# The gate of a mixture-of-experts layer computed with tokens as weights and 8 moving columns

## The chip, the cores and the metric

The kernel runs on one NeuronCore of one Trainium2 chip. The metric is device time in microseconds, the median of several runs. TensorE multiplies matrices (its loads of weights are shown as an engine of their own, PEld, since they overlap its products), VectorE (DVE) and ScalarE (ACT) work on elements, GpSimd (POOL) too, and SyncE (SP) issues DMAs.

## The reference

An attention with two kinds of local mask gives 2304 tokens of 512 channels. A mixture of 8 experts follows, whose weights P come from a gate, and then a squared-ReLU layer. The part that the change touches is the gate:

```python
def _moe_ref(x, w_gate, w1, w2):
    N, D = x.shape                      # 2304, 512
    E = w_gate.shape[1]                 # 8
    logits = x @ w_gate
    logits = logits - logits.max()
    P = np.exp(logits)
    for _ in range(8):
        P /= P.sum(1, keepdims=True) + 1e-09
        P /= P.sum(0, keepdims=True) + 1e-09
        P *= N / E
    out = np.zeros((N, D), dtype=np.float32)
    for e in range(E):
        h = np.maximum(x @ w1[e], 0.0)
        ye = h @ w2[e]
        out += P[:, e:e + 1] * ye
    return out
```

## The kernel before

The attention's output stays in SBUF as `xf`, with the channels on the partitions: 128 partitions, 4 channel tiles (`KC`), 2304 tokens, in float32. The attention is a software pipeline of 28 slots (`slot`, line 754). In slot i TensorE gets the scores of group i (`s`, line 297), the products with the values of group i-3 (`xt`, line 349), the transposes of group i-2 (`pt`, line 334) and then a few filler products (`warm_up`, line 752, 128x512). ScalarE copies `xt` out of PSUM into `xf` (line 377), and the next slot's `xt` products wait for those copies, as there are two PSUM buffers.

Every engine's queue has the order in which the code is written (`manual_schedule`); no planner reorders it. The gate is a generator: each `next` records one piece. In the attention loop a gate over 512 tokens is made in slots 10, 16 and 22, so its first piece stands behind the fillers of that slot, and its second piece behind the fillers of the next slot. The tokens from 1536 on have two more gates, of 512 and 256 tokens, after the loop: their pieces stand around the first two units of the expert stage (`l1_pair`, whose products are line 477).

A gate's first piece computes the logits with the channels' gate weights loaded: for each of the 4 channel tiles the 8 gate columns, padded to 32, are the weights, and 512 tokens move. The four products go to four strips of 32 partitions of one PSUM bank, so there are four partial sums with the expert on the partition. VectorE copies the bank to SBUF (`lt`). The second piece transposes 128 tokens at a time with `ident`, and VectorE adds the four partial sums in one reduction into `ptile`, which has a token on each partition and 18 x 8 logits behind it. `sinkhorn` reads `ptile`; its steps are recorded after the units of the first expert steps, and one of its products, line 435, has a 128x128 matrix of ones as weights and 8 moving columns in float32.

The rest of the kernel, from some 117 us on, is a long sequence of expert and feed-forward products (lines 477, 604, 635) that neither the gate nor the change touches.

Of the kernel before, what the change touches and what calls it, by code (L numbers as in the profile page):

```python
# [9 lines left out]
F32 = mybir.dt.float32  # L10
# [4 lines left out]
ALU = mybir.AluOpType  # L15
AX = mybir.AxisListType
# [4 lines left out]
E, FE, FF = 8, 1024, 2048  # L21
# [9 lines left out]
KC = DM // 128  # L31
# [16 lines left out]
def tile_kernel(ctx: ExitStack, tc: tile.TileContext, a):  # L48
    nc = tc.nc
    out = a["out"]  # L50
# [8 lines left out]
    xfp = att.enter_context(tc.tile_pool(name="xfp", bufs=1))  # L59
    qkv = att.enter_context(tc.tile_pool(name="qkv", bufs=2))  # L60
    at = att.enter_context(tc.tile_pool(name="at", bufs=2))
# [7 lines left out]
    ptile = big.tile([128, NCH, E], F32, name="ptile")  # L69

    xf = xfp.tile([128, KC, NTOK], F32, name="xf")

    ident = const.tile([128, 128], F32, name="ident")
    mask = xfp.tile([128, 4 * GB, KB], F32, name="mask")
    wg = xfp.tile([128, KC, 32], F32, name="wg")
    warm = xfp.tile([128, 128], F32, name="warm")
    guard = xfp.tile([128, GB, 1], F32, name="guard")

# [5 lines left out]
    bufs = {"s": 2, "xt": 2, "pt": 1, "mm": 3}  # L84

    def bank(tag):
        return psum.tile([128, 512], F32, tag=tag, name=tag, bufs=bufs[tag])
# [290 lines left out]


    def gate(t0, n):  # L380
        ps = bank("mm")
        for kc in range(KC):
            nc.tensor.matmul(
                ps[32 * kc:32 * kc + 32, :n], wg[:, kc], xf[:, kc, t0:t0 + n], start=True, stop=True
            )
        lt = at.tile([128, 512], F32, tag="lt", name="lt", bufs=1)
        nc.vector.tensor_copy(lt[:, :n], ps[:, :n])
        yield
        ps2 = bank("mm")
        nch = n // 128  # L390
        for c in range(nch):
            nc.tensor.transpose(ps2[:, c * 128:(c + 1) * 128], lt[:, c * 128:(c + 1) * 128], ident)
        c0 = t0 // 128
        nc.vector.tensor_reduce(
            out=ptile[:, c0:c0 + nch, :],
            in_=ps2[:, :n].rearrange("p (c k q) -> p c q k", k=KC, q=32)[:, :, :E, :],
            axis=AX.X,
            op=ALU.add,
        )
        yield  # L400

    def sinkhorn():
# [272 lines left out]
    with tc.manual_schedule():  # L675
# [14 lines left out]
        ps = psum.tile([128, 512], F32, tag="s", name="s")  # L690
# [88 lines left out]
        for i in range(NG + LAG):  # L779
            slot(i)  # L780
            if i % per == LAG and i > per:
                t = i // per - 1
                gates.append(gate(t * 512, 512))
            if gates:
                try:
                    next(gates[0])
                except StopIteration:
                    gates.pop(0)
            for i0, z in ops:
                if i >= i0:  # L790
                    next(z, None)
            if per + 2 <= i and prep0:
                prep0.pop(0)()
            if i == 3 * per + LAG:
                nc.sync.dma_start(x_dram[:, :, :early], xf[:, :, PAIRS[1]:3 * S])
# [7 lines left out]
        )  # L803
        first_units = l1_pair(0)
        gates += [gate(t0, n) for t0, n in ((1536, 512), (2048, 256))]
        next(gates[0])
        run(first_units[0])
# [70 lines left out]
def _layout(x):  # L878
    q, k, v = x["q"], x["k"], x["v"]

    def order(z):
        lo = z[:, :4]
        hi = z[:, 4:].reshape(B, 4, S // DIL, DIL, D).transpose(0, 1, 3, 2, 4).reshape(B, 4, S, D)
        return np.stack([lo, hi], axis=1)

    qo, ko, vo = order(q), order(k), order(v)

    def pairs(z):
        return z.reshape(B, 2, 2, 2, S, D).transpose(0, 1, 3, 5, 2, 4)

    qs = pairs(qo).reshape(B, 2, 128, 2, NM, QC).transpose(0, 1, 4, 2, 3, 5)
    kz = pairs(ko).reshape(B, 2, 128, 2, S)
    kz = np.concatenate([np.zeros((B, 2, 128, 2, PAD), kz.dtype), kz], axis=-1)
    ks = np.stack([kz[..., m * QC:m * QC + KCOLS] for m in range(NM)], axis=2)

    vp = np.concatenate([np.zeros((B, 2, 4, PAD, D), v.dtype), vo], axis=3)
    vt = np.stack([vp[:, :, :, j * QB:j * QB + KB] for j in range(NB)], axis=3)
    vt = vt.reshape(B, 2, 4, NM, 2, GB // 2, KB, D).transpose(0, 1, 3, 4, 6, 5, 2, 7)
    vt = vt.reshape(B, 2, NM, 128, GB // 2, 4 * D)

    def first(w, n):
        return w.reshape(KC, 128, n, FC, 128).transpose(2, 1, 3, 0, 4).reshape(n, 128, KC * FB)

    def second(w, n):
        return w.reshape(n, FC, 128, DM).transpose(0, 2, 1, 3).reshape(n, 128, FC * DM)

    w1 = np.concatenate([first(x["moe_w1"][e], SPE) for e in range(E)])
    w2 = np.concatenate([second(x["moe_w2"][e], SPE) for e in range(E)])
    kk = np.arange(KB)[None, :]
    qq = np.arange(QB)[:, None]  # L910
    band = (kk > qq) & (kk <= qq + PAD)

    def split_at(o):
        return band & ((qq < o) | (kk >= PAD + o))

    first_block, split, after_split = split_at(0), split_at(QB // 2), band & (kk >= QB // 2)
    masks = [
        z[3 * (k % 2) + k // 2]
        for z in (
            [first_block] + [band] * 5,  # L920
            [first_block, band, band, band, split, after_split],
            [band, band, band, first_block, band, band],
            [band, split, after_split, band, band, band],
        )
        for k in range(GB)
    ]
    arrays = {
        "q": qs,
        "k": ks,
        "v": vt,  # L930
        "w_gate": np.pad(x["moe_w_gate"].reshape(KC, 128, E).transpose(1, 0, 2), ((0, 0), (0, 0), (0, 32 - E))),
        "w1": w1,
        "w2": w2,
        "w_in": first(x["moe2_w_in"], NS2),
        "w_out": second(x["moe2_w_out"], NS2),
        "mask": np.tile(np.stack([np.where(m, 0.0, NEG).astype(np.float32) for m in masks], axis=1), (4, 1, 1)),
        "ident": np.eye(128, dtype=np.float32),
    }
    arrays = {n: np.ascontiguousarray(z) for n, z in arrays.items()}
    for n in ("w_in", "w_out"):  # L940
        arrays[n] = arrays[n].view(np.int64)
    return arrays
# [16 lines left out]
```

## Time and profile before

| | |
|---|---|
| median of 3 runs | 2044.98 us (2043.14 to 2047.37) |
| the profiled execution | 2052.68 us |
| its span, first to last instruction | 2050.9 us |
| TensorE: products, of the span | 2017.1 us, 98% |
| TensorE: loads of weights | 1663.0 us, 81% |
| VectorE | 1558.3 us, 76% |
| ScalarE | 720.4 us, 35% |
| GpSimd | 386.6 us, 19% |
| mean granted clock of TensorE | 0.993 of full speed |

The profile is of one execution. An engine's busy time counts the stretches in which it has an instruction in flight. Products are pipelined: the time from one's start to the start of the next says more of the pace than the length of one. A float32 product of the gate or of the attention shows two records of loads and two of products, so four of the gate's products read x8. The granted clock has two levels here, 2.4 GHz (1.00) and 1.2 GHz (0.50).

### The profile page before, as it was taken

To read this page: it belongs to the slowest core of one execution; us is meant where nothing else is said; L and a number is where in the kernel's file an instruction comes from. 1 tells how busy PE (TensorE), PEld (TensorE's weight loads), DVE (VectorE), ACT (ScalarE), POOL (GpSimd) and SP (SyncE) were. 2 spreads that over 40 slices of the span, in tenths; PEclk is the share of its full clock that TensorE was granted. 3 is DMA by queue.
4 is the path that set the end of the run, shared out by engine and by line. 5 is a ranking of instruction groups with operands and counts; after the bars stand their busy time and mean duration, and the time that the engine had idled before them with its cause. 6 is when DMAs were issued, how large, how long until landed. Compare 5 with 4: busy or idle time off the path is not lost.

```text
span 2050.9 us, 28660 instructions
## 1 busy us (share of the span) xinstructions
PE 2017.1 (98%) x11584; PEld 1663.0 (81%) x11584; DVE 1558.3 (76%) x2435; ACT 720.4 (35%) x1149; POOL 386.6 (19%) x416
## 2 busy tenths in 40 slices
PE   9999999999999999999999999999999999999999
PEld 7778888888888888888888888888888878887887
DVE  4766777777777777778888888888887786678676
ACT  3443222223322232223433333333333344344542
POOL 3522311111011111111311212121211231123120
PEclk8899999999999999999999999999999999999999
DMA  8512121222212121213222322323221231112111
GB/s 279 177 65 61 52 57 57 62 65 62 65 50 61 56 61 47 70 57 98 103 93 87 87 85 71 97 78 98 82 86 59 75 111 42 39 54 103 62 42 52
DMA packets 71509, 159.35 MB, mean 78 GB/s; under 512 B 6336, under 2 KB 33104, under 8 KB 71376
## 3 DMA queue, kind: packets, MB, share of 16 engines
q1 hardware_dynamic: 71376, 157.52, 23.8%
q8 instruction: 91, 1.49, 0.3%
q14 instruction: 42, 0.34, 0.1%
HBM read 137.49 MB, written 20.00 MB: 77 GB/s over the span
## 4 chain that ended last, share of the span: by engine, by line
PE 87%; DVE 10%; ACT 2%; issue 1%; POOL 0%; ACTq 0%; DVEq 0%; POOLq 0%
PE mm L635 42%; PE pt L477 16%; PE s L477 10%; PE xt L477 9%; PE mm L604 5%; DVE acc L647 3%; PE xt L349 2%; DVE gl L511 2%; DVE g L525 1%; DVE suml L135 1%; PE mm L752 1%; PE s L297 1%; PE pt L334 1%; DVE x_lo L212 1%; DVE s L584 1%
## 5 line engine op out<-in xcount | busy, mean ns | idle before, releaser
L647 DVE TENSOR_TENSOR acc<-mm,acc 128x512 f32<-128x512 f32 x746 | 473.2, 642 | 188.4 <-PE mm L635 184.4
L635 PE MATMUL mm<-gl,w2h 128*128 128x512 f32 x1024 | 403.3, 394 | 0.0
L635 PE MATMUL mm<-gh,w2h 128*128 128x512 f32 x1024 | 402.3, 393 | 0.8 <-DVE acc L647 0.7
L635 PE MATMUL mm<-gh,w2l 128*128 128x512 f32 x1024 | 402.8, 393 | 0.0
L533 ACT CAST gh<-g 128x512 fp32r<-128x512 f32 x308 | 191.5, 622 | 592.8 <-DVE g L525 592.6
L144 POOL TENSOR_TENSOR sums<-raw 128x256 f32<-128x256 f32 x80 | 66.2, 827 | 1466.7 <-DVE suml L135 1423.8
L635 PEld LDWEIGHTS mm<-gh,w2h 128*128 128x128 f32 x1024 | 192.4, 188 | 46.8 <-DVE acc L647 1.6
L635 PEld LDWEIGHTS mm<-gl,w2h 128*128 128x128 f32 x1024 | 192.3, 188 | 43.9
L635 PEld LDWEIGHTS mm<-gh,w2l 128*128 128x128 f32 x1024 | 192.3, 188 | 43.7
L511 DVE TENSOR_TENSOR gl<-g,gh 128x512 fp32r<-128x512 f32 x308 | 223.8, 731 | 0.9 <-ACT gh L533 0.9
L525 DVE SCALAR_TENSOR_TENSOR g<-s,pp 128x512 f32<-128x512 f32 x183 | 128.8, 704 | 111.6 <-PE s L477 109.4
L477 PE MATMUL pt<-x_hi,sumh 128*128 128x512 f32 x320 | 126.4, 395 | 3.7 <-ACT s L570 3.7
L477 PE MATMUL s<-x_hi,blkh 128*128 128x512 f32 x320 | 126.3, 395 | 1.0 <-ACT pt L558 1.0
L477 PE MATMUL xt<-x_hi,sumh 128*128 128x512 f32 x320 | 126.6, 396 | 0.0
L477 PE MATMUL xt<-x_lo,sumh 128*128 128x512 f32 x320 | 126.0, 394 | 0.0
L477 PE MATMUL pt<-x_lo,sumh 128*128 128x512 f32 x320 | 125.9, 393 | 0.0
L477 PE MATMUL xt<-x_hi,suml 128*128 128x512 f32 x320 | 125.9, 393 | 0.0
L477 PE MATMUL pt<-x_hi,suml 128*128 128x512 f32 x320 | 125.8, 393 | 0.0
L477 PE MATMUL s<-x_lo,blkh 128*128 128x512 f32 x320 | 125.8, 393 | 0.0
L477 PE MATMUL s<-x_hi,blkl 128*128 128x512 f32 x320 | 125.5, 392 | 0.0
L135 DVE TENSOR_TENSOR w2l<-raw,w2h 128x1024 fp32r<-128x1024 f32 x80 | 100.7, 1259 | 14.9 <-ACT w2h L131 14.9
L533 ACT CAST sgh<-g 128x256 fp32r<-128x256 f32 x74 | 29.9, 406 | 219.0 <-DVE g L525 219.0
(151 smaller groups left out, 3970.3 us busy)
## 6 DMA issues: line engine op xcount, KB each, us to landing
raw<-in_w SPq DMA_DIRECT2D x128, 512.0 KB, 3.5
raw<-w SPq DMA_DIRECT2D x32, 512.0 KB, 3.4
v<-in_v SPq DMA_DIRECT2D x24, 384.0 KB, 3.9
pp<-p_dram SPq DMA_DIRECT2D x32, 256.0 KB, 5.6
xb<-in_w_in SPq DMA_DIRECT2D x16, 512.0 KB, 4.7
w<-xb SPq DMA_DIRECT2D x32, 256.0 KB, 2.3
xb<-in_w_out SPq DMA_DIRECT2D x16, 512.0 KB, 4.7
k<-in_k SPq DMA_DIRECT2D x24, 224.0 KB, 4.6
```

What stands on the lines that cost most here:

```text
L135: nc.vector.tensor_tensor(out=w[1], in0=src, in1=w[0].bitcast(F32), op=ALU.subtract)
L144: tt(out=c(sums, 0), in0=c(raw1, 2), in1=c(raw1, 3), op=ALU.add)
L212: return lambda: nc.vector.tensor_tensor(out=x_lo[:, k, j], in0=z, in1=x_hi[:, k, j].bitcast(F32), op=ALU.subtract)
L297: nc.tensor.matmul(ps[QB * head:QB * head + QB, 2 * (g % 3) + g // 3, :], qt[rows, pr, g * QB:g * QB + QB], kt[rows, pr, g * QB:g * QB + K ...
L349: nc.tensor.matmul(xt[D * h:D * h + D, pr, c * QB:c * QB + QB], vt[keys, c, head * D:head * D + D], pt[keys, c * 128 + head * QB:c * 128 + ...
L477: nc.tensor.matmul(ps, w[:, c], z[:, x, j], start=start and k == 0, stop=stop and k == 5, skip_group_check=True)
L511: nc.vector.tensor_tensor(out=glo, in0=z, in1=ghi.bitcast(F32), op=ALU.subtract)
L525: nc.vector.scalar_tensor_tensor(out=held["g"], in0=src, scalar=0.0, in1=held["r"], op0=ALU.max, op1=ALU.mult)
L533: after(k + 1, lambda: nc.scalar.copy(ghi, held["g"]))
L604: nc.tensor.matmul(ps, w[:, c], z[:, kc], start=k == 0, stop=k == 3 * KC - 1)
L635: nc.tensor.matmul(ps, lhsT, rhs, start=k == 0, stop=k == 3 * FC - 1)
L647: nc.vector.tensor_tensor(out=dst, in0=ps, in1=dst, op=ALU.add)
```

## The change

The gate's product is turned round. For 128 tokens at a time a channel tile of `xf` is loaded as the weights (128 channels by 128 tokens), and the 8 gate columns of that channel tile move. The four channel tiles accumulate in PSUM, and the result has the token on the partition already. So the copy to `lt`, the transposes, the second PSUM bank and the reduction over the four partial sums go; one VectorE copy of 8 columns per 128 tokens takes `ptile` out of PSUM. The gate is one piece instead of two. The gate weights are no longer padded to 32 columns.

```diff
-    wg = xfp.tile([128, KC, 32], F32, name="wg")
+    wg = xfp.tile([128, KC, E], F32, name="wg")
...
     def gate(t0, n):
-        ps = bank("mm")
-        for kc in range(KC):
-            nc.tensor.matmul(
-                ps[32 * kc:32 * kc + 32, :n], wg[:, kc], xf[:, kc, t0:t0 + n], start=True, stop=True
-            )
-        lt = at.tile([128, 512], F32, tag="lt", name="lt", bufs=1)
-        nc.vector.tensor_copy(lt[:, :n], ps[:, :n])
-        yield
-        ps2 = bank("mm")
-        nch = n // 128
+
+        c0, nch = t0 // 128, n // 128
+        ps = bank("mm")[:, :nch * E]
         for c in range(nch):
-            nc.tensor.transpose(ps2[:, c * 128:(c + 1) * 128], lt[:, c * 128:(c + 1) * 128], ident)
-        c0 = t0 // 128
-        nc.vector.tensor_reduce(
-            out=ptile[:, c0:c0 + nch, :],
-            in_=ps2[:, :n].rearrange("p (c k q) -> p c q k", k=KC, q=32)[:, :, :E, :],
-            axis=AX.X,
-            op=ALU.add,
-        )
+            for kc in range(KC):
+                nc.tensor.matmul(
+                    ps[:, c * E:c * E + E],
+                    xf[:, kc, t0 + c * 128:t0 + c * 128 + 128],
+                    wg[:, kc],
+                    start=kc == 0,
+                    stop=kc == KC - 1,
+                )
+        nc.vector.tensor_copy(ptile[:, c0:c0 + nch, :], ps.rearrange("p (c e) -> p c e", e=E))
         yield
...
-        "w_gate": np.pad(x["moe_w_gate"].reshape(KC, 128, E).transpose(1, 0, 2), ((0, 0), (0, 0), (0, 32 - E))),
+        "w_gate": x["moe_w_gate"].reshape(KC, 128, E).transpose(1, 0, 2),
```

In the kernel after the change all lines behind the gate stand 6 higher: the fillers are line 746, the expert products line 471, the gate's products line 386.

TensorE's queue around the second gate (slots 16 to 18), before. A row names the output and, behind the arrow, the two operands, then the size of one output and how often the row stands in a run. s, xt and pt are the PSUM tiles of the attention, mm that of fillers and gates, xr and wr the fillers' operands:

```order
L752 MATMUL mm<-xr,wr 128x512 x3
L383 MATMUL mm<-xf,wg 32x512 x4
L297 MATMUL s<-k,q 32x64 x24
L349 MATMUL xt<-pts,v 64x32 x24
L334 MATMUL pt<-ident,ms 128x128 x3
L752 MATMUL mm<-xr,wr 128x512 x3
L392 MATMUL mm<-ident,lt 128x128 x4
```

The same place after:

```order
L746 MATMUL mm<-xr,wr 128x512 x3
L386 MATMUL mm<-wg,xf 128x8 x16
L297 MATMUL s<-k,q 32x64 x24
L349 MATMUL xt<-pts,v 64x32 x24
L334 MATMUL pt<-ident,ms 128x128 x3
L746 MATMUL mm<-xr,wr 128x512 x3
```

The four wide products have become sixteen with 8 columns in the same place, and the four transposes one slot later are gone.

TensorE's queue around the last two gates, at the start of the expert stage, before:

```order
L801 MATMUL pt<-x_hi,blkh_139 128x512
L383 MATMUL mm<-xf,wg 32x512 x4
L477 MATMUL s<-x_hi,blkh_139 128x512
...
L392 MATMUL mm<-ident,lt 128x128 x4
L383 MATMUL mm<-xf,wg 32x256 x4
L477 MATMUL xt<-x_hi,sumh_141 128x512
...
L392 MATMUL mm<-ident,lt 128x128 x2
L477 MATMUL s<-x_hi,blkh_139 128x512
```

And after:

```order
L795 MATMUL pt<-x_hi,blkh_139 128x512
L386 MATMUL mm<-wg,xf 128x8 x16
L471 MATMUL s<-x_hi,blkh_139 128x512
...
L386 MATMUL mm<-wg,xf 128x8 x8
L471 MATMUL xt<-x_hi,sumh_141 128x512
...
L471 MATMUL s<-x_hi,blkh_139 128x512
```

Six expert products stand between the two gates and six behind the second, as before; both groups of transposes are gone.

VectorE's queue at the second gate, before:

```order
L326 RECIPROCAL rs<-rs 128x6
L387 COPY lt<-mm 128x512
L706 TENSOR_TENSOR x_lo<-xf,x_hi 128x512
L310 SCALAR_TENSOR_TENSOR ms<-s,mask 128x384
...
L394 TENSOR_REDUCE ptile<-mm 128x32
L706 TENSOR_TENSOR x_lo<-xb,x_hi 128x512
```

And after:

```order
L326 RECIPROCAL rs<-rs 128x6
L393 COPY ptile<-mm 128x32
L700 TENSOR_TENSOR x_lo<-xf,x_hi 128x512
L310 SCALAR_TENSOR_TENSOR ms<-s,mask 128x384
...
L700 TENSOR_TENSOR x_lo<-xb,x_hi 128x512
```

The small copy stands where the large one stood, ahead of the x_lo subtraction and the next masked scores; the reduction is gone.

## Rows read from the trace of the kernel before

**Rows 1.** The page: busy time of each engine, and TensorE's clock in tenths.

```profile
PE 2017.1 (98%) x11584; PEld 1663.0 (81%) x11584; DVE 1558.3 (76%) x2435; ACT 720.4 (35%) x1149; POOL 386.6 (19%) x416
...
PEclk8899999999999999999999999999999999999999
```

**Rows 2.** Timeline, TensorE, gate 0: start us, length us, engine, line, operation, [wait].

```profile
49.91 1.88 PE L383 MATMUL mm<-xf,wg 128*32 128x512 f32 x8
51.72 0.87 PE L297 MATMUL s<-k,q 64*32 64x64 f32 x48
```

**Rows 3.** Timeline, TensorE, gate 1 and the slot behind it.

```profile
78.21 1.07 PE L383 MATMUL mm<-xf,wg 128*32 128x512 f32 x8
79.21 0.88 PE L297 MATMUL s<-k,q 64*32 64x64 f32 x48
80.01 1.39 PE L349 MATMUL xt<-pts,v 64*64 64x32 f32 x48
...
82.41 0.60 PE L392 MATMUL mm<-ident,lt 128*128 128x128 f32 x4
82.94 0.87 PE L297 MATMUL s<-k,q 64*32 64x64 f32 x48
83.94 1.39 PE L349 MATMUL xt<-pts,v 64*64 64x32 f32 x48
```

**Rows 4.** Timeline, TensorE, gates 3 and 4 at the expert stage's start.

```profile
116.45 1.06 PE L383 MATMUL mm<-xf,wg 128*32 128x512 f32 x8
117.45 0.50 PE L477 MATMUL s<-x_hi,blkh 128*128 128x512 f32 x1
...
118.25 0.40 PE L477 MATMUL s<-x_hi,blkh 128*128 128x512 f32 x1
118.48 0.39 PE L477 MATMUL s<-x_lo,blkh 128*128 128x512 f32 x1
...
118.95 0.60 PE L392 MATMUL mm<-ident,lt 128*128 128x128 f32 x4
119.48 0.64 PE L383 MATMUL mm<-xf,wg 128*32 128x256 f32 x8
120.05 0.50 PE L477 MATMUL xt<-x_hi,sumh 128*128 128x512 f32 x1
```

**Rows 5.** Timeline, TensorE: starts of xt products, one a slot.

```profile
61.04 1.76 PE L349 MATMUL xt<-pts,v 64*64 64x32 f32 x48 [1.42 <-ACT xf L377]
...
66.28 2.38 PE L349 MATMUL xt<-pts,v 64*64 64x32 f32 x48
...
72.13 1.39 PE L349 MATMUL xt<-pts,v 64*64 64x32 f32 x48
...
87.85 1.39 PE L349 MATMUL xt<-pts,v 64*64 64x32 f32 x48 [0.54 <-ACT xf L377]
```

**Rows 6.** Timeline, loads of weights: 64x64 tiles, then one product of line 435.

```profile
80.01 1.28 PEld L349 LDWEIGHTS xt<-pts,v 64*64 64x64 f32 x48
...
139.26 0.30 PEld L435 LDWEIGHTS mm<-scs,xb 128*128 128x128 f32 x2 [1.40 <-DVE scs L429]
139.48 0.19 PEld L477 LDWEIGHTS pt<-x_hi,sumh 128*128 128x128 f32 x1
```

**Rows 7.** By tile, VectorE: the gate's copy and reduction, ns min/median/max.

```profile
L387 DVE COPY lt<-mm x5: 427/692/692, 51.9 to 120.2; 128x512 f32<-128x512 f32 x4, 128x256 f32<-128x256 f32 x1
...
L394 DVE TENSOR_REDUCE ptile<-mm x5: 225/291/292, 55.6 to 122.0; 128x32 f32<-128x128 f32 x4, 128x16 f32<-128x64 f32 x1
```

**Rows 8.** By stretch: length, busy us (instructions) per engine, granted clock, DMA share, GB/s.

```profile
37.95:51.60 13.65, 13.65 (x213) 9.64 (x212) 5.17 (x12) 5.77 (x15) 7.35 (x10) 0.50 0.56 182
51.60:61.85 10.25, 8.83 (x294) 7.55 (x292) 8.97 (x18) 4.97 (x12) 3.60 (x4) 1.00 0.41 123
61.85:72.10 10.25, 10.25 (x180) 8.31 (x172) 6.25 (x11) 3.80 (x10) 3.87 (x4) 0.50 0.74 251
72.10:116.40 44.30, 40.44 (x1061) 32.03 (x1057) 32.05 (x62) 21.74 (x58) 31.30 (x31) 1.00 0.37 117
```

## Prediction

> **What bounds the kernel now.** I read the page's first two parts first: TensorE has work in 98% of the span, at nearly the full clock [rows 1]. So time added to its queue is mostly time added to the kernel, unless it stands where TensorE waits anyway. The gate is a tiny part of that queue, so the whole question lies in the first 125 us, and there I read the timeline of TensorE around the gates. I number them 0 to 4 in order of time.
>
> Gate 0 runs at 1.2 GHz: its products start at 49.91 and the next product at 51.72, 1.81 us [rows 2]. Gate 1 runs at 2.4 GHz: 78.21 to 79.21 is 1.00 us, and its four transposes one slot later, 82.41 to 82.94, are 0.53 us [rows 3]. I take gate 2 as a copy of it. Gate 3 takes 116.45 to 117.45, 1.00 us, its transposes 118.95 to 119.48, 0.53 us, and gate 4, with half the tokens, 119.48 to 120.05, 0.57 us [rows 4]. Four products of 512 columns fit in 1.00 us only because the four 32-wide column tiles stream side by side. All gates with their transposes (0.2 us for gate 4's two, an estimate from the 0.53 us of four) make 1.8 + 3 x 1.0 + 0.6 + 4 x 0.53 + 0.2 = 7.7 us of TensorE.
>
> What bounds a slot of the attention is read from the start of its xt products. From 83.94 to 87.85 is 3.91 us, and at the end of it TensorE waits 0.54 us for ScalarE's copies [rows 3, 5]: TensorE and the chain through ScalarE are close together there. In a slot with a gate that wait is gone already (no wait stands at 80.01) [rows 3], so every further microsecond of gate lengthens the slot.
>
> **The change part by part.** *The new products.* A gate of 512 tokens is now 16 products with 128x128 weights and 8 moving columns, and gate 4 is 8 of them. The kernel before has exactly this form in one place, line 435: weights 128x128 in float32, 8 columns. One such product shows two loads; they begin at 139.26, and the next instruction's load begins at 139.48 [rows 6], so the pace is 0.11 us a load and 0.22 us a product. That is with columns that take next to nothing, so the loads are the pace. A full gate is then 16 x 0.22 = 3.5 us, gate 4 is 1.8 us, and all 72 products are 15.8 us at 2.4 GHz. The other bound is the nearest faster row: 48 loads of 64x64 tiles in 1.28 us, 27 ns each [rows 6], or 53 ns for twice the columns, which would make a full gate 1.7 us. I take 0.11, since it is the same form; the 64x64 loads go to two tiles in turn, and 16 full-width products have only one place to go. At 1.2 GHz I double it, as gate 0 took 1.81 where gate 1 took 1.00: 7.0 us.
>
> *On the path.* Gate 0, if the clock is low as in this trace: 7.0 - 1.8 = +5.2 us (at 2.4 GHz only 3.5 - 1.8 = +1.7). Gates 1 and 2: 3.5 - 1.0 = +2.5 each. Gate 3: +2.5. Gate 4: 1.8 - 0.6 = +1.2. Together +13.9.
>
> *The transposes that go.* Behind gates 1 and 2 they return nothing: the slot that holds them, 80.01 to 83.94, is 3.93 us, and the next one without them 3.91 [rows 3, 5]. They lie where TensorE would wait. Behind gates 3 and 4 no such wait follows, so 0.5 + 0.2 = -0.7 us.
>
> *VectorE.* Each gate loses a copy of 692 ns and a reduction of 291 ns, and gains a copy of 32 columns [rows 7]. That copy lies between nothing and the 0.29 us of the reduction with the same output; I take 0.2, nearer to the reduction, so some 0.8 us less. It counts only where VectorE's chain sets the end, which is after gate 0: there the xt products at 61.04 waited 1.42 us [rows 5]. I put -0.8 there. The new copy waits for the longer gate, and queued behind it on VectorE are the x_lo subtraction and the next slot's masked scores; these scores need products that stand behind the gate on TensorE anyway, so the wait adds nothing of its own. The gate's weights arrive by a DMA a quarter the size, some 30 us before use: nothing. One PSUM bank less per gate changes which bank comes next, and no row shows a wait for one: nothing.
>
> Sum at the clock of the trace: 13.9 - 0.7 - 0.8 = +12.4 us.
>
> *The clock.* This is the uncertain term. In the attention TensorE was at 1.2 GHz from 37.95 to 51.60 and from 61.85 to 72.10, and at 2.4 GHz between and after [rows 8]. What went before: ahead of the fall near 61.85 stands the wait of 1.42 us at 61.04, ahead of 64x64 tile products with 32 columns [rows 5]; ahead of the rise near 51.60 stand gate 0's products, 512 columns each [rows 2]. And from 37.95 to 51.60 TensorE was busy for all of the 13.65 us, with 9.64 us of loads, and still stayed low [rows 8]. So instructions in flight alone didn't bring the clock back here. The new gate puts 3.5 us of loads with 8-column products where long products were. I expect it to act on the clock as the waits did: gate 0 no longer brings the clock up, and gates 1, 2 and 3 each bring it down.
>
> The Trainium skill, page "TensorE: Matmul & The Clock Gate", Part 1, describes the gate as following how busy TensorE has recently been, and its table under "Why this matters for your kernels" names idle gaps as what costs the clock. By that rule the new gates, which never leave TensorE idle, cost no clock, and the sum would stay at +12.4 instead of what follows. The stretch at 1.2 GHz with TensorE busy throughout doesn't fit the plain reading; whether it holds for a gate made of loads, no run here shows.
>
> The price: a slot at 1.2 GHz is 66.28 to 72.13, 5.85 us, against 3.91, so +1.9 each [rows 5]. A low stretch here lasted 10 to 14 us, which I take as two slots, +3.9. After gate 0: +3.9. After gates 1 and 2: +7.8. After gate 3: gate 4 twice as long, +1.8, and 12 products of the next stage at twice the 0.23 us from one to the next, +2.8 [rows 4]; +4.6. To take off: the low stretch from 61.85, whose wait at 61.04 no longer comes up if TensorE is the slow one there; it cost 5.24 + 5.85 - 2 x 3.9 = 3.3. Clock term: 3.9 + 7.8 + 4.6 - 3.3 = +13.0. Both ends: -3.3 (no new fall, and the wait at 61.04 gone) and +35.6 (rival three).
>
> **Sum:** 12.4 + 13.0 = +25.4 us. The profiled execution took 2052.68 us (span 2050.9, 1.8 around it), 7.7 above the median of 2044.98, more than the three runs differ among themselves. Low stretches that differ from run to run could make that up. I add the difference to the median: 2044.98 + 25 = 2070 us.
>
> **The rivals.** *One: the clock holds.* Gates 1 to 3 leave it at 2.4 GHz. For it: TensorE isn't idle in them, and the fall near 61.85 came with a wait. Against it: the busy stretch at 1.2 GHz. It gives +12.4, about 2057 us, or 2054 if gate 0 runs at 2.4 GHz (3.5 less). This is what that page of the Trainium skill would give.
>
> *Two: not slower.* The loads of a stream of full-width products follow each other at the pace of the narrow tiles, 53 ns, and the clock isn't disturbed. Then 144 loads take 7.7 us, what the gates take now, and with 0.8 us of VectorE gone the kernel is where it was, 2045 us. It decides at 0.05 us a load: above that the change loses. Against it stands line 435, where three loads in a row start 0.11 us apart [rows 6].
>
> *Three: the clock doesn't come back in the attention.* Once low at gate 0 it stays low up to the next stage. From 51.60 to 116.40 some 54 us were at 2.4 GHz [rows 8], about 11 full slots and 2 short ones without scores. At +1.9 and an estimated +1.5 these are +24; gates 1 and 2 at 7.0 instead of 3.5 are +7, and what follows gate 3 is +4.6 as above, +35.6 in all. With the 12.4 that is +48, 2093 us. Against it: the clock rose within 14 us in both stretches.
>
> **How the numbers follow.** Forecast (falls at the gates, with recovery) 0.62; rival one 0.22; rival two 0.07; rival three 0.09. The time is the forecast's, 2070; its own range is 2060 to 2084 (two falls fewer or three more, at 4 us each). The range reaches down to rival one with gate 0 at full clock and leaves out rival two and most of three: 2052 to 2086. A measurement of this kernel can tell about 0.2%, 4 us, from no change. Faster needs more than rival two gives: 0.02. Same is rival two's rest and a cheap rival one: 0.06. Slower: 0.92.
>
> **What would show it.** In the profile after: loads on the new gate line 0.11 us apart, 3.5 us for a gate at 2.4 GHz (if 0.05, rival two). The granted clock by stretch: 1.2 GHz through gate 0 and two slots on, and again after gates 1, 2 and 3 (if 2.4 throughout after gate 1, rival one). Slots without a transpose no shorter than 3.9 us. From the sinkhorn steps on, everything as before, only shifted. The prediction is wrong if the shift at the end of the attention isn't the whole difference, which would mean a wait I haven't seen.

## The result, and the profile after

The changed kernel takes 2077.96 us in the median (2074.74 to 2079.73, four runs) against 2046.17 (2043.14 to 2048.59, four runs): 31.8 us more. The recorded ratio is 1.0146, 95% interval 1.0129 to 1.0163, which is 26 to 33 us; here and below the ratios are worked out from the runs and are not the quotients of the medians (that is 1.0155 here). The forecast was 2070 in a range of 2052 to 2086, slower. Two executions further down took far longer at a lower clock than the others of their kernel, 3292.0 us at a mean of 0.555 and 2100.17 us at 0.970, and are named where they matter.

The page of the changed kernel begins so (busy time per engine, then the granted clock in 40 slices):

```profile
span 2075.8 us, 28825 instructions
...
PE 2040.4 (98%) x11670; PEld 1690.5 (81%) x11670; DVE 1552.7 (75%) x2430; ACT 720.3 (35%) x1149; POOL 385.2 (19%) x416
...
PEclk9869999999999999999999999999999999999999
```

TensorE's share stays at 98%, as in [rows 1]: a share of busy time doesn't show this loss at all. The third slice of the clock does. By stretches of the granted clock (length, busy us and instructions of PE, PEld, DVE, ACT, POOL, then clock, DMA share, GB/s), answering [rows 8]:

```profile
4.17:48.54 44.37, 37.44 (x1008) 30.77 (x1006) 23.84 (x52) 15.11 (x40) 20.11 (x25) 1.00 0.89 310
48.54:62.20 13.66, 13.66 (x243) 11.67 (x246) 7.62 (x14) 3.78 (x9) 3.88 (x4) 0.50 0.43 137
62.20:79.26 17.06, 15.23 (x410) 13.06 (x402) 12.16 (x23) 8.90 (x25) 9.64 (x10) 1.00 0.64 209
79.26:89.50 10.24, 10.24 (x174) 9.06 (x174) 4.07 (x9) 1.85 (x5) 3.17 (x3) 0.50 0.27 94
89.50:109.98 20.48, 18.90 (x487) 16.28 (x486) 13.13 (x29) 10.18 (x27) 14.32 (x14) 1.00 0.40 126
109.98:147.53 37.55, 36.79 (x330) 31.98 (x330) 8.01 (x18) 7.34 (x18) 7.07 (x8) 0.50 0.09 33
```

Three stretches at 1.2 GHz, 61 us in all, each with TensorE busy all or nearly all of it. They begin where the gates stand. TensorE's timeline at the gates and the xt products behind them, answering [rows 2 to 5]:

```profile
45.60 4.15 PE L386 MATMUL mm<-wg,xf 128*128 128x8 f32 x32
49.68 1.51 PE L297 MATMUL s<-k,q 64*32 64x64 f32 x48
51.12 2.38 PE L349 MATMUL xt<-pts,v 64*64 64x32 f32 x48
...
56.97 2.38 PE L349 MATMUL xt<-pts,v 64*64 64x32 f32 x48
...
76.97 4.73 PE L386 MATMUL mm<-wg,xf 128*128 128x8 f32 x32
81.62 1.51 PE L297 MATMUL s<-k,q 64*32 64x64 f32 x48
...
106.63 3.76 PE L386 MATMUL mm<-wg,xf 128*128 128x8 f32 x32
110.32 1.51 PE L297 MATMUL s<-k,q 64*32 64x64 f32 x48
111.76 2.38 PE L349 MATMUL xt<-pts,v 64*64 64x32 f32 x48
...
116.74 2.38 PE L349 MATMUL xt<-pts,v 64*64 64x32 f32 x48 [0.49 <-ACT xf L377]
...
131.37 6.83 PE L386 MATMUL mm<-wg,xf 128*128 128x8 f32 x32
138.05 0.77 PE L471 MATMUL s<-x_hi,blkh 128*128 128x512 f32 x1
...
140.76 3.42 PE L386 MATMUL mm<-wg,xf 128*128 128x8 f32 x16
144.02 0.77 PE L471 MATMUL xt<-x_hi,sumh 128*128 128x512 f32 x1
```

Gate 0 entered at 2.4 GHz and the clock fell within it (48.54). Gate 1 is 4.65 us long because the clock fell within it too (79.26). Gate 2 runs almost whole at 2.4 GHz, 3.69 us, and the clock falls at its end (109.98). Gate 3 runs at 1.2 GHz, 6.68 us, and gate 4 too, 3.26 us. From gate 3's first product to the product behind gate 4 is 12.65 us, where before it was 3.60 [rows 4].

Behind that nothing changes. The next line is the changed kernel's 1900 us from 160 on, and the one in the second fence 1900 us of the kernel before, begun 22.4 us earlier:

```profile
160.00:2060.00 1900.00, 1881.83 (x8922) 1556.27 (x8921) 1468.05 (x2258) 664.76 (x1015) 326.78 (x348) 1.00 0.22 69
```

```profile
137.60:2037.60 1900.00, 1881.60 (x8921) 1555.88 (x8920) 1467.82 (x2252) 662.96 (x1012) 326.99 (x348) 1.00 0.22 69
```

The two stretches begin 2.7 us of work apart, as the two queues lie some 25 us apart by then, but both hold only the products behind the gates, and TensorE's busy time in them differs by 0.2 us. The product behind gate 4 stands 23.97 us later than before (144.02 against 120.05), and the ends of the two spans are 24.9 us apart: all of the loss is made in the first 150 us.

The two profiled executions differ by only 24.9 us (2077.57 - 2052.68), less than the medians do. The runs' mean granted clocks say why: with each run it is listed, and (1 - clock) x 2 x span is its time at 1.2 GHz (0.001 is 4 us). The profiled execution of before has 0.993, some 27 to 31 us, of which [rows 8] shows 24. Of the 46 runs of before that were made on three chips along with the experiments 40 have 0.996 to 0.999, 4 to 16 us. The execution I predicted from had more of the low clock than most. Part of it stood ahead of the gates, where the change does nothing: gate 0 began at 49.91 in it and at 45.60 in the changed kernel's profile.

### The profile page after: what moved, and what is told of

It is laid out like the page before. It is cut to its first block, busy times and chain, and to the rows that moved or that the text cites. A ratio compares the mean times of both kernels' runs of the same rounds, so it can differ in the third digit from the quotient of the medians.

```text
span 2075.8 us, 28825 instructions
## 1 busy us (share of the span) xinstructions
PE 2040.4 (98%) x11670; PEld 1690.5 (81%) x11670; DVE 1552.7 (75%) x2430; ACT 720.3 (35%) x1149; POOL 385.2 (19%) x416
## 4 chain that ended last, share of the span: by engine, by line
PE 87%; DVE 10%; ACT 2%; issue 1%; DMA 1%; SPq 0%; ACTq 0%; DVEq 0%
PE mm L629 41%; PE pt L471 15%; PE s L471 10%; PE xt L471 9%; PE mm L598 5%; DVE acc L641 3%; PE xt L349 2%; DVE gl L505 2%; DVE g L519 1%; DVE suml L135 1%; PE mm L386 1%; PE mm L746 1%; PE s L297 1%; PE pt L334 1%; DVE x_lo L212 1%
```

## Experiments

Each stands beside runs of the kernel before on the same chip, with medians of 2044.5 to 2046.1. Two theories are to be told apart: that the loss is the queue's time alone (72 products at the pace of their loads), or that the larger part is the clock that falls with these products.

### The same time in the queue, with long products

```diff
-        ps = bank("mm")[:, :nch * E]
+        full = bank("mm")
+        ps = full[:, :nch * E]
...
-                nc.tensor.matmul(
-                    ps[:, c * E:c * E + E],
-                    xf[:, kc, t0 + c * 128:t0 + c * 128 + 128],
-                    wg[:, kc],
-                    start=kc == 0,
-                    stop=kc == KC - 1,
-                )
+                nc.tensor.matmul(full, wr, xr, start=True, stop=True)
```

`full` is the gate's PSUM bank, `wr` and `xr` are the fillers' operands.

> The changed kernel with each 8-column product of a gate replaced by a filler product of 512 columns into the same PSUM bank, 16 of them a gate (8 in the last), so TensorE's queue is held for about the same 3.5 us a gate at 2.4 GHz (16 x 0.215). The gate's logits are left out: ptile gets zeros. Theory (the clock is the larger term: gates of loads with 8 columns bring TensorE to 1.2 GHz): the granted clock stays at 2.4 GHz from the first gate to the expert stage, and the kernel lands at the gates' own time over before, 15.8 - 7.7 = +8 us, 2054 (2046 to 2060). Rival (the time is the queue's, the clock has no part): as the changed kernel, 2078, with the same clock stretches.

Measured: 2059.59, ratio 1.0062 (1.0043 to 1.0081), +13.5 us. Stretches of the clock:

```profile
41.35:61.83 20.48, 18.64 (x470) 15.51 (x469) 14.19 (x30) 9.09 (x22) 9.47 (x12) 1.00 0.59 185
61.83:75.49 13.66, 13.66 (x247) 11.04 (x249) 7.56 (x13) 5.66 (x15) 5.88 (x6) 0.50 0.61 198
75.49:140.00 64.51, 59.42 (x1063) 48.04 (x1056) 34.28 (x73) 26.26 (x63) 27.89 (x28) 1.00 0.30 97
```

and what stands ahead of the one fall (TensorE's timeline):

```profile
59.88 1.33 PE L349 MATMUL xt<-pts,v 64*64 64x32 f32 x46 [1.40 <-ACT xf L377]
```

Five gates, each holding the queue for some 3.7 us as in the changed kernel, and no fall at any of them: the one in this stretch follows the old wait of 1.4 us, as in [rows 5]. Ahead of gate 2 both kernels have the same waits, 0.46 and 0.21 us in the two slots before it, so a wait doesn't make the difference there; ahead of gate 0 they differ (0.79 us in the changed kernel at 44.05, 0.17 here). Less than half of the 31.8 us is the queue's; 18 us go when the same queue time is spent in long products. The edit changes more than the columns, though: a gate here has 16 loads instead of 32, and its operands are the fillers' (`xr` is zeros). Which of these keeps the clock up, this run doesn't tell. It is +13.5 rather than +8, and its runs' clock of 0.995 against before's 0.997 in the median is part of that.

### More work behind the gate's products

```diff
+        fill = bank("mm")
...
+                if kc % 2:
+                    nc.tensor.matmul(fill, wr, xr, start=True, stop=True)
```

> The changed kernel with one more product, a 512-column filler, behind every second product of a gate: 36 fillers more, about 0.2 us each, some of it over the next load. Theory (clock): more work, yet faster than the changed kernel; a gate is 4.5 to 5 us and holds the clock at 2.4 GHz, 2078 + 6 - 20 = 2064 (2056 to 2070). Rival (the clock has no part): 2078 + 6 = 2084.

Measured: 2081.85, ratio 1.0167 (1.0144 to 1.0190). The expectation missed; the time is nearer to the rival's 2084. The low stretches:

```profile
51.50:65.15 13.65, 13.65 (x237) 11.24 (x239) 7.62 (x14) 3.63 (x8) 3.88 (x4) 0.50 0.41 132
...
85.63:92.46 6.83, 6.83 (x147) 5.84 (x146) 3.27 (x7) 1.85 (x5) 3.17 (x3) 0.50 0.31 101
...
133.42:147.07 13.65, 13.65 (x45) 11.73 (x45) 1.82 (x5) 1.53 (x2) 0.00 (x0) 0.50 0.00 0
```

In this execution, the shortest of the four (clock 0.991, the others 0.985 to 0.987), they are 34 us instead of 61, and gate 2 passes without a fall, but in or right behind gates 0, 1 and 3 the clock still falls: long products between the narrow ones didn't hold it. A gate became 5.4 us instead of 3.5: the fillers hid no load. What they gave back in clock they took in the queue. This run alone doesn't separate the theories.

### One end of the change at a time

Gates 0 to 2 in the new form, 3 and 4 in the old (`gate_old` is the gate of the kernel before):

```diff
-        gates += [gate(t0, n) for t0, n in ((1536, 512), (2048, 256))]
+        gates += [gate_old(t0, n) for t0, n in ((1536, 512), (2048, 256))]
```

> Gates 0 to 2 in the new form, gates 3 and 4 at the start of the expert stage in the old form with their transposes. Theory (clock): the low stretch that begins at gate 2 goes on to the expert stage, but the old gates with 512 columns bring the clock back early; the last gates cost about 5 us instead of 12.7, so 2078 - 7 = 2071 (2066 to 2074). Rival (loads alone): the last gates give back 3.5 + 1.8 - 2.3 = 3 us, 2075.

Measured: 2071.52, ratio 1.0119 (1.0088 to 1.0151), +25.4 us: near the theory's 2071, but the four runs (2065.5 to 2075.2) reach the rival's 2075 as well. The clock at the end of the attention:

```profile
108.94:132.83 23.89, 23.12 (x281) 18.00 (x280) 6.19 (x13) 5.83 (x16) 7.07 (x8) 0.50 0.13 47
132.83:150.00 17.17, 16.09 (x91) 12.17 (x88) 10.63 (x22) 8.24 (x13) 0.00 (x0) 1.00 0.12 37
```

The old gate 3 began at 131.48, and the clock is back 1.4 us later; with the new one it came back 16 us after the gate's start.

The other half, gates 0 to 2 old, 3 and 4 new:

```diff
-                gates.append(gate(t * 512, 512))
+                gates.append(gate_old(t * 512, 512))
```

> Gates 0 to 2 in the old form, gates 3 and 4 in the new one. Theory: the loads' own time in the last two gates is 3.5 + 1.8 - 2.3 = 3.0 us, and gate 3 brings the clock down within the expert stage's first units, up to 4.6 more: 2053 (2048 to 2056). Rival (no fall there, as the stage's own products are dense): 2049.

Measured: 2052.23, ratio 1.0035 (1.0019 to 1.0050), +7.7 us: near the theory's 2053, though the interval reaches down to the rival's 2049. The timeline, of the shortest of its executions (2046.88), decides:

```profile
106.55 3.83 PE L408 MATMUL mm<-wg,xf 128*128 128x8 f32 x32
110.23 0.77 PE L493 MATMUL s<-x_hi,blkh 128*128 128x512 f32 x1
110.81 0.63 PE L493 MATMUL s<-x_lo,blkh 128*128 128x512 f32 x1
111.23 0.63 PE L493 MATMUL s<-x_hi,blkl 128*128 128x512 f32 x1
```

The expert products behind gate 3 are 0.43 us apart, twice the 0.23 of [rows 4]: the clock fell in gate 3 here as well, though it was at 2.4 GHz before. The two halves add up within the runs' spread, 25.4 + 7.7 = 33.1 against 31.8.

### The loads spread over slots

```diff
     def gate(t0, n):
 
-        c0, nch = t0 // 128, n // 128
-        ps = bank("mm")[:, :nch * E]
-        for c in range(nch):
+        for c in range(t0 // 128, (t0 + n) // 128):
+            ps = bank("mm")[:, :E]
             for kc in range(KC):
                 nc.tensor.matmul(
...
+                    ps, xf[:, kc, c * 128:c * 128 + 128], wg[:, kc], start=kc == 0, stop=kc == KC - 1
                 )
-        nc.vector.tensor_copy(ptile[:, c0:c0 + nch, :], ps.rearrange("p (c e) -> p c e", e=E))
-        yield
+            nc.vector.tensor_copy(ptile[:, c, :], ps)
+            yield
```

> The changed kernel with a gate in pieces of 128 tokens (4 products, 8 loads, 0.9 us), one piece a slot in the attention and one behind each of the first units of the expert stage, the same 72 products in all and one small copy a piece. Theory (it is the unbroken 3.5 us of loads that bring the clock down, and a slot's wait hides half of a piece): the queue's part falls from 13.5 us (what the run with fillers in place of the products added) to 9, and most of the clock's part goes: 2046 + 9 + 4 = 2059 (2052 to 2066). Rival (the loads themselves pull the clock, however they are spread): 2078 - 4 = 2074.

Measured: 2076.04, ratio 1.0185 (1.0121 to 1.0248), where my theory said 2059 and the rival 2074. Without the execution of 2100.17 us the median is 2073.10; either way it is the rival's figure, with runs from 2065.84 on. Stretches of the clock and a slot of TensorE's timeline:

```profile
44.71:82.26 37.55, 37.55 (x598) 33.67 (x598) 16.58 (x36) 12.86 (x32) 10.41 (x13) 0.50 0.45 147
82.26:126.00 43.74, 42.36 (x1093) 38.24 (x1090) 31.91 (x66) 21.82 (x58) 30.61 (x31) 1.00 0.39 118
```

```profile
46.68 2.38 PE L349 MATMUL xt<-pts,v 64*64 64x32 f32 x48
...
50.96 1.71 PE L385 MATMUL mm<-wg,xf 128*128 128x8 f32 x8
52.60 1.51 PE L297 MATMUL s<-k,q 64*32 64x64 f32 x48
54.04 2.16 PE L349 MATMUL xt<-pts,v 64*64 64x32 f32 x44
```

A slot with a piece of gate 0 in it is 7.36 us at 1.2 GHz. The clock was low when the first piece came (it fell at 44.71, behind a stop of 0.80 us) and stayed low until behind the last one, where with the gate of before it rose within the gate [rows 8]. So part of my theory falls: in this execution the clock didn't rise among the pieces either. The other part stands in this trace: the pieces of gates 1 and 2, behind 82.26, start no fall. But this execution is the shortest of the four (2065.84, clock 0.988). The others have 0.984 and less, and where they were low no trace shows.

### More fillers

Two, three or four fillers a slot become four in all:

```diff
-            warm_up(4 if i < 6 else 2 if i < per + 4 else 3)
+            warm_up(4)
```

With the spread gate:

> The spread gate of the run above and four fillers in every slot. Theory (clock): with 512-column products in every slot the clock holds throughout, so only the loads' own time is left, 2046 - 6 + 10 = 2050 (2044 to 2056). Rival (queue alone): 2059 + 5 = 2064 or more.

Measured: 2058.95, ratio 1.0066 (1.0041 to 1.0090). Twenty-six products more, and 17 us less than without them (14 without the execution of 2100.17 us; all on the same chip, and the longest of these runs, 2065.41, is below the shortest of those, 2065.84). In the profiled execution the clock holds for nearly all of it:

```profile
24.92:120.49 95.57, 93.18 (x2222) 82.47 (x2220) 61.94 (x131) 42.92 (x110) 50.04 (x55) 1.00 0.53 172
120.49:123.90 3.41, 3.41 (x11) 2.83 (x11) 1.63 (x4) 0.00 (x0) 0.00 (x0) 0.50 0.01 2
```

The rival had it slower than the spread gate alone. The runs' clocks go from 0.998 (2052.9) to 0.991 (2065.4), so in some executions it still fell, which is part of why it lies above my 2050; even at 0.998 the runs are at 2052.94 and 2055.36.

With the gate in one piece:

> The changed kernel, gates in one piece, with four fillers in every slot. Theory (clock): the gates still bring the clock down, but with more 512-column products a slot it comes back sooner and isn't low at gates 3 and 4 from before; mean clock about 0.992 instead of 0.985: 2046 + 10 (loads' own time) + 8 = 2064 (2056 to 2071), faster than the changed kernel with 26 products more. Rival (queue alone): 2078 + 1 to 5 = 2081.

Measured: 2073.19, ratio 1.0130 (1.0102 to 1.0159), 9 us above the expectation. It is 5 us below the changed kernel, with more work, but the two were run on different chips, and the two ratios' intervals overlap (1.0129 to 1.0163 for the changed kernel): that it is faster isn't shown. Its profiled execution, the shortest of the four, has five low stretches from 51 to 140, 37.6 us in all instead of 61; four fillers a slot don't prevent them.

With the gate of before:

> The kernel before with four filler products in every slot of the attention instead of two (slots 6 to 9) or three (from 10): 26 products of 512 columns more, 5.6 us of TensorE. Theory (the clock is a cost in the kernel before too, and a slot's wait of 0.46 us covers a filler more): the granted clock stays at 2.4 GHz from slot 6 on, the two low stretches go, 2046 - 6 = 2040 (2035 to 2046). Rival (TensorE's queue is all that counts): 2046 + 5 = 2051.

Measured: 2046.53 against 2045.81, ratio 1.0000 (0.9989 to 1.0010). The clock held (no low stretch behind 24.01 in the profiled execution), but there was little to gain: I had taken the 27 us of low clock in the profile of before for its usual state, and at the 0.34 us per us that is worked out below the usual 4 to 16 us are worth 1 to 5 us, no more than the 26 fillers may cost.

### Narrow strips, and no gate at all

A load of 128 tokens takes the array's whole width (128*128 in the rows). In strips of 32 tokens four loads go to four strips of it (128*32):

```diff
-                    ps[:, c * E:c * E + E],
-                    xf[:, kc, t0 + c * 128:t0 + c * 128 + 128],
+                    ps[32 * j:32 * j + 32, c * E:c * E + E],
+                    xf[:, kc, tok:tok + 32],
```

Here j goes from 0 to 3 and `tok` is t0 + 128 c + 32 j.

> The changed kernel with the 128 tokens of a product cut into four strips of 32: four loads of 32 columns and four 8-column products into four partition strips of the same PSUM columns, otherwise the same. Theory (a full-width load has one place to go, strips load side by side, as the scores' 48 loads of 32 columns in 0.71 us do at 15 ns each): 128 loads a gate take 1 to 2 us instead of 3.5; fewer microseconds without long products, so fewer falls of the clock: 2050 (2042 to 2060). Rival (the loads' columns follow each other whatever their strips): 3.5 us a gate and 2078.

Measured: 2061.52, ratio 1.0077 (1.0055 to 1.0099): just above the expected range of 2042 to 2060, and far below the rival's 2078. TensorE's timeline at gate 2 and the low stretch that follows:

```profile
102.41 1.26 PE L388 MATMUL mm<-wg,xf 128*32 128x8 f32 x128
103.60 0.41 PE L297 MATMUL s<-k,q 64*32 64x64 f32 x13
106.35 1.27 PE L297 MATMUL s<-k,q 64*32 64x64 f32 x35 [2.34 <-issue]
```

```profile
106.09:133.39 27.30, 26.28 (x451) 21.25 (x451) 5.76 (x13) 7.06 (x18) 7.07 (x8) 0.50 0.13 46
```

The loads do run side by side: 128 in 1.2 us, a third of the full-width form. But 64 products are many instructions, and behind them TensorE stands 2.34 us for nothing that the profile shows; what its queue was short of isn't settled. The clock falls at that gap's end, so in this run the gap and the missing long products can't be told apart as its cause.

Spread and with four fillers:

> The turned product in strips of 32 tokens (16 products of 32x8 for 128 tokens), spread over slots, with four fillers in every slot. Theory: the strips' loads take some 0.35 us a piece, which a slot's wait covers, the transposes and the large copies are gone, and the clock holds: 2038 (2032 to 2046), faster than both kernels. Rival (issue gaps as with the unspread strips, 1 to 2 us a gate, and a clock that falls): 2055.

Measured: 2048.37 against 2045.81, ratio 1.0011 (1.0002 to 1.0020). The expectation missed by 10 us. The clock held (0.997 to 1.000 in the runs), and a piece takes 0.36 us (72.68 to 73.04 in its timeline), but TensorE again stands in slots behind the pieces, twice for 0.37 us, and the 27 us of low clock that I meant to save are seldom there, which is the larger part. TensorE's timeline at one piece:

```profile
72.68 0.44 PE L387 MATMUL mm<-wg,xf 128*32 128x8 f32 x32
73.04 0.87 PE L297 MATMUL s<-k,q 64*32 64x64 f32 x48
73.85 0.89 PE L349 MATMUL xt<-pts,v 64*64 64x32 f32 x29
75.11 0.77 PE L349 MATMUL xt<-pts,v 64*64 64x32 f32 x19 [0.37 <-issue]
```

It is the best form of the turned product that I ran, and it doesn't beat the kernel before, with four fillers (2046.53) or without.

No products for the gate:

```diff
-        c0, nch = t0 // 128, n // 128
-        ps = bank("mm")[:, :nch * E]
-        for c in range(nch):
...
-        nc.vector.tensor_copy(ptile[:, c0:c0 + nch, :], ps.rearrange("p (c e) -> p c e", e=E))
+        nc.vector.memset(ptile[:, t0 // 128:(t0 + n) // 128, :], 0.0)
```

> No gate products at all: the gate's piece is a memset of its part of ptile, so the logits are left out; everything else as in the changed kernel. Theory (the gate of before pays part of its way by holding the clock with 512 columns): about 5.5 us of TensorE's path go, but the granted clock's mean falls below before's 0.997, and some 5 us come back: 2046 (2041 to 2052). Rival (queue alone): 2040.5, with before's clock.

Measured: 2047.02 against 2044.51, ratio 0.9997 (0.9980 to 1.0015). This is near the theory's 2046, not the rival's 2040.5: without any gate the kernel isn't faster. The only trace is of the execution of 3292.0 us, so where the clock was low can't be seen. The other runs go from 2039.35 at a mean clock of 0.999 to 2050.44 at 0.991, and the kernel before's on the same chip have 0.996 to 1.000 in all but one. At the same clock of 0.999 it is 2039.4 against 2043.3 to 2044.5, so 4 to 5 us of gate are gone; in the median the clock takes them back. It also prices the clock: 11.1 us between clocks that are 0.008 apart, or 33 us at 1.2 GHz, is 0.34 us lost per us (0.3 to 0.4, as the clocks have three decimals).

## Why the prediction was right, point by point

**The pace of the loads: right.** 0.11 us from line 435. Gate 2, nearly all at 2.4 GHz, has 32 loads in 3.69 us, 0.115 each, and gate 3 at 1.2 GHz 32 in 6.68, 0.21. Gate 2's loads in the timeline:

```profile
106.40 3.90 PEld L386 LDWEIGHTS mm<-wg,xf 128*128 128x128 f32 x32
```

Rival two (0.053) is out for full-width loads. In strips its rate is passed: 128 loads of a quarter of the width in 1.19 us (102.41 to 103.60), 0.037 for 128 columns.

**The queue's term: right in size.** At 2.4 GHz throughout the prediction had 12.4 - 3.5 = +8.9. The run with long products is +13.5; at 0.34 us per us, its 20 us at 1.2 GHz (clock 0.995) against 12 of before (0.997) are worth about 3, so +10 to +11 is the queue's.

**The clock: right in sign and place, too small.** Counting gate 0's extra as clock, the prediction had 25.4 - 8.9 = +16.5; the rest of the measured 31.8 is about +21. The runs' own clocks give +18: 0.982 to 0.986 is some 64 us at 1.2 GHz, against some 10 of before, at 0.34 us per us. The 3 us between the two stay open. Gate 2 of the kernel before stands at

```profile
101.57 1.07 PE L383 MATMUL mm<-xf,wg 128*32 128x512 f32 x8
```

and so the starts of the gates' products, in [rows 2 to 4] and in TensorE's timeline of the changed kernel, give each stage of the two profiled executions. The forecast is what the prediction's terms come to in that stage:

| from start to start | before | after | more | forecast |
|---|---|---|---|---|
| gate 0 to gate 1 | 28.30 | 31.37 | +3.1 | +5.0 |
| gate 1 to gate 2 | 23.36 | 29.66 | +6.3 | +6.4 |
| gate 2 to gate 3 | 14.88 | 24.74 | +9.9 | +6.4 |
| gate 3 to the product behind gate 4 | 3.60 | 12.65 | +9.1 | +6.4 |

Three steps of the clock term failed. First, "two slots" for every low stretch. After gate 1 it held (10.24 us). After gate 2 it did not: the clock didn't rise before gate 3, and the stretch is 37.55 us long. One slot there has scores and the three behind it have none; why the clock stayed low, no run shows. That is rival three, but for the last gates alone. Gate 3 was priced at +2.5 and cost 6.68 - 1.00 = 5.7. Second, the subtraction of 3.3 for a low stretch of before: it stands in the profiled execution, but seldom in the median of the runs. Third, the same for gate 0 at 1.2 GHz: in the changed kernel's profiled execution gate 0 took 4.08, not 7.0. Second and third nearly cancel, by luck, so the shortfall is the first. It is luck too that the forecast's +25.4 is so near the 24.9 us between the two profiled executions: from gate 0 on they differ by 29.2, and 4.3 come off for the low clock that before had ahead of gate 0.

What it is in these gates that costs the clock (the few columns, the loads, the operands) the runs don't separate.

**Idle gaps.** In the changed kernel TensorE was busy 36.79 of 37.55 us and stayed at 1.2 GHz, and the clock fell in gates 0 to 2 without a wait in them. The Trainium skill (page "TensorE: Matmul & The Clock Gate", "Why this matters for your kernels") names idle gaps as what costs the clock. By that rule the kernel would have come to rival one's 2057, and the run with long products, which also never idles in the gates, would have matched the changed kernel. The trace differs, and the measurement decides.

**VectorE: the copy was right, the gain was not there.** The new copy is 191 ns in the median, I had 0.2. But the -0.8 us at the slot behind gate 0 failed: in the run with long products, which has the same small copies, the wait there is 1.40 us, as it was 1.42 [rows 5]. What ends it is ScalarE's own queue. In the kernel before:

```profile
59.11 1.05 ACT L131 CAST sumh<-sums 128x1024 fp32r<-128x1024 f32 x1
...
60.48 0.85 ACT L377 COPY xf<-xt 128x192 f32<-128x192 f32 x3
```

The copies of `xt` stand behind a cast of 1.05 us that has nothing to do with the gate, and in the run with long products the same cast stands there (57.95, copies at 59.32). The prediction took the wait for one of VectorE's chain.

**The transposes behind gates 1 and 2: nearly right.** In the run with long products the slot behind gate 1 is 3.64 us (82.68 to 86.32) against 3.93, so they returned 0.3 us, not nothing.

**The shift is the whole difference: right.** The 1900 us behind it differ by 0.2 us of TensorE's busy time.

## What to carry to other kernels

Before a product is turned round, count its loads and not only its columns: 32 full-width loads at 0.11 us took 3.5 us where 512 columns in four strips side by side took 1.0. In this stage the clock fell in three of the changed kernel's gates and in none of those with long products of the same time, so price what is taken away as well as what is added; a run with the same queue time in long products separates the two terms at once. And read the mean clock of the timed runs beside that of the profile before using a low stretch as a cost.

## What the runs showed of the hardware that I had not expected

The clock stayed at 1.2 GHz for 37.55 us with TensorE busy for nearly all of it in the changed kernel and for all of it in the spread one. Twenty-six added products of 512 columns made the kernel with the spread gate 14 to 17 us faster, and taking the gate away altogether made none (0.9997). Behind 64 small products in a row TensorE stood 2.34 us with nothing to wait for that the profile shows.
